# Softmax attention beside a long convolution on one core: groups by quarter of the heads, then by query block

## The chip, the cores and the metric

The kernel runs on one core of a Trainium2 chip. What is measured is device time in microseconds (us) of one launch, from the first to the last instruction with what lies around them; 859.79 us is the median of three runs (858.05 to 861.04). The core has a TensorE (PE) for matmuls into eight PSUM banks, a VectorE (DVE), a ScalarE (ACT), a GpSimd (POOL), a SyncE (SP) that mainly issues transfers, and 16 DMA engines.

## What is computed

Two independent parts write the two halves of the output rows. Part A is attention with 32 heads of 16 channels over 2048 positions; part B is a causal long convolution per channel.

```python
# A: x [2048,512], wqkv [512,1536], wo [512,512]; 32 heads of 16
qkv = (x @ wqkv) -> q, k, v per head
scores = einsum("bhqd,bhkd->bhqk", q, k) * 16 ** -0.5
p = softmax(scores, axis=-1)
o = einsum("bhqk,bhkd->bhqd", p, v)
a = o.reshape(1, 2048, 512) @ wo
# B: q, k, v [2048,512]; shift_k [512,4]; ssm_k [512,2048]; ssm_D [512]
k_shift[s] = sum over m of k[s - m] * shift_k[:, m]
kv = k_shift * v
y = causal convolution of kv with ssm_k along the positions (the reference uses an FFT) + kv * ssm_D
b = q * y
out = concatenate([a, b], axis=-1)
```

## The kernel before

**An order planned while the program is written.** One Python loop at the end of the function runs over steps T. In each step it emits instructions for PE, ACT, DVE, POOL and the DMA queues through objects of class `Eng` and the helper `dma` (its issues all show as L227). Those keep estimated clocks (`pe.t`, `dve.t`, `done`), from which the planner decides what fits where. On the chip the engines follow the order that was written, held only by semaphores: PE, ACT and DVE each run their instructions strictly in that order, so a waiting instruction holds up all behind it.

**Attention.** The 2048 x 2048 scores of each head are cut into blocks of 128 keys x 512 queries: 32 heads x 16 key tiles x 4 query blocks = 2048 blocks. A group is one query block and four heads that sit in the four 32-row strips of PE: 32 groups of 64 blocks. Before, the groups run by query block (`qb`) first and by group of heads (`g`, 8 of them) within it, and the first two groups are interleaved. A step T takes two or three blocks: `emit_qk` puts the score matmuls (L548) into two or three PSUM banks (0 to 2 and 3 to 5 by turns), and ACT takes the exponentials of the step in one instruction (L559) into a ring of five `PT` buffers. Two or three steps later `emit_pv` (L641) multiplies them with the values `VAF`, which carry columns of ones for the softmax sum, and accumulates a group in bank `PVB`. At a group's end DVE transposes it (L705), divides (L712, L716) and, for each pair of groups, transposes back into `OTN` (L729).

**Blocks on DVE.** From step `T_DVE` = 56 on, the third block of a three-bank step may have its exponential on DVE instead (`dve_block`, `exp_on_dve`): one L595, three L602 and one L607, each 128 x 512. The step's ACT instruction is then two blocks wide. A block is only given to DVE when its estimated backlog is at most `BACKLOG` = 3.9 us.

**Projections.** `pe_unit` makes pieces of work in one PSUM bank, emitted in halves, and `evac_unit` copies them out by DVE: `q` (L339, two masked copies L385), `k` (L348, L390), `v` (L368, L414; one key tile for all heads), `kv` (the convolution's shifted and multiplied input, L360, L400). Before, all values, keys and the first query block are projected in the first `N_EARLY` = 184 steps by the list `early`; in these, every second step has two banks only and the units use the free one, bank 5. Later units go to 25 openings of five steps, 21 steps apart from step 190, of which the first, third and fifth step have two banks (`T_SLOT`, `SLOT`, `N_SLOT`, `opens`, `slots`). The number of steps is fixed by this: 184 steps hold 92 x 2 + 92 x 3 = 460 blocks, the openings have 75 two-bank steps, the last 14 blocks go by twos in 7 steps, and the rest needs 475 steps of three, in sum 741.

**Convolution.** `ssm_k` is reversed by DVE (`kz_turn`, L435) and stored to DRAM (`kz_store`). `load_wr` reads from there, for each of 128 quartets of channels, four 128 x 2048 Toeplitz rows of 512 KB into a filter slot of `WR`; there are three slots (`R_W` = 12 rows). `conv_lags` (L815) does up to six lags a step in bank `BGB`, DVE copies the result (L830), PE turns it (L841) and DVE multiplies with q (L850). The transposed loads of `B_k` that `kv` needs are `load_kt(0..2)`; the rows for `load_kt(2)` come free after the last `k` unit.

**Output.** `op_mm`/`op_out` (L760, L769) multiply `OTN` with `WO` and store through POOL's queue. `warm_up` (L1025) adds at most one filler matmul per step, of up to four times 128 columns, where PE would otherwise have been less than `BUSY` = 0.75 busy over the last `WINDOW` = 3.4 us by the planner's clock.

Of the kernel before, what the change touches and what calls it, by code (L numbers as in the profile page):

```python
# [11 lines left out]
S = 2048  # L12
# [9 lines left out]
VROW = 592  # L22
# [7 lines left out]
R_W = 12  # L30
R_PT = 5
R_O = 8
# [4 lines left out]
N_EARLY = 184  # L37
# [21 lines left out]
T_DVE = 56  # L59
T_SLOT = 190  # L60
SLOT = 21
N_SLOT = 25
# [5 lines left out]
BACKLOG = 3.9  # L68
MARGIN = 0.35
EARLY_MARGIN = 0.25  # L70
KV_DUE = 300
# [4 lines left out]
FILL_GAP = 0.25  # L76
RATE = 3.4
# [59 lines left out]
def bass_concat_heads__mha_block__ssm_conv_h3__prompt_kernel(  # L137
# [24 lines left out]
    def sb(name, shape, dt=BF16):  # L162
# [4 lines left out]
    KTo = sb("KTo", [128, 4, S])  # L167
    QTF = sb("QT", [128, 2 * NG * QB + 2 * LEFT])
    QT = QTF[:, 0:2 * NG * QB].rearrange("p (b g f) -> p b g f", b=2, g=NG)
    VAF = sb("VAF", [128, KT, VROW])  # L170
# [9 lines left out]
    WKV = sb("WKV", [128, 8 * D + LEFT])  # L180
    OTN = sb("OTN", [128, R_O, QB])
# [15 lines left out]
    WO = WV  # L197
    VST = [x.rearrange("p (t d) -> p t d", t=NB)
           for x in (WR[:, 8, :], WR[:, 9, :], OUTA[:, :, :].rearrange("p r d -> p (r d)"), VS2[:, :])]
# [3 lines left out]
           QTF[:, NG * QB:NG * QB + LKR].rearrange("p (c s) -> p c s", c=1),  # L203
           WKV[:, 4 * D:4 * D + LKR].rearrange("p (c s) -> p c s", c=1)]
    KT_OF = [(0, 0), (0, 1), (1, 0), (2, 0)]
    DG = OTN[:, 4:8, :].rearrange("p t d -> p (t d)").rearrange("p (c m d) -> p c m d", c=4, m=4)
    KZN = [QTF[:, NG * QB:NG * QB + 2 * S].rearrange("p (c s) -> p c s", c=2),
# [53 lines left out]
    d_w = [DmaSem(sem(f"d_w{i}")) for i in range(5)]  # L261
# [19 lines left out]
    h_wv = dma(act, d_w[2], WV, wview[:, :, 2 * D:3 * D])  # L281
    load_x(1)
    h_wq.append(dma(act, d_w[3], WQ[:, :, 128:D], wview[:, :, 128:D], kb=384))
    h_wk.append(dma(act, d_w[4], WK[:, :, 128:D], wview[:, :, D + 128:2 * D], kb=384))
    h_shk = dma(act, d_tap, SHK[:, :, :], B_shift_k.rearrange("(c p) m -> p c m", p=128), kb=4)
# [4 lines left out]
    load_x(2)  # L290
    load_x(3)
    h_vn, h_kt, h_kt0 = [], {}, {}
    for c in range(4):
        src = bass.AP(tensor=v2.tensor, offset=v2[128 * (NB - 1), 128 * c].offset, ap=[[D, 128], [-128 * D, NB], [1, 128]])
        h_vn.append(dma(sp, d_kv[3 + c], VST[c], src, kb=1024))
# [16 lines left out]
    vones = VAF[:, :, 0:H * VW].rearrange("p k (h e) -> p k h e", e=VW)  # L312
    pool.op(lambda e: e.memset(vones[:, :, :, DH:VW], 1.0))
    h_vaf1 = pool.op(lambda e: e.memset(VAF[:, :, H * VW:VROW], 1.0))
# [3 lines left out]

    bank_free = {b: None for b in range(8)}
    h_q, h_k, h_v = {}, {}, {}  # L320
    def unit_deps(u):
        if u[0] == "q":
            return h_x[u[1]] + [h_wq[min(u[2], 1)]]
        if u[0] == "k":
            return h_x[u[2]] + [h_wk[min(u[1], 1)]]
        if u[0] == "kv":
            return [h_kt[KT_OF[u[1]][0]], h_dg[0]]
        return h_x[u[1] // 4] + [h_wv]

    def pe_unit(u, bank, dcs=(0, 1, 2, 3)):  # L330
# [3 lines left out]
        if kind == "q":  # L334
            _, qb, o = u
# [27 lines left out]
        else:  # L363
            _, kt = u
            deps += h_x[kt // 4] + [h_wv]

            def mm(e, dc):
                return e.matmul(PS[:, bank, :], lhsT=xT[:, dc, kt * 128:(kt + 1) * 128], rhs=WV[:, dc, :],  # L368
                                start=(dc == 0), stop=(dc == 3))

        def fn(e):
            ins = None
            for dc in dcs:
                ins = mm(e, dc)
            return ins
        return pe.op(fn, deps, us=(0.105 + mm_us * len(dcs), 0.235 + mm_us * len(dcs)),
                     run=mm_run * len(dcs))

    def evac_unit(u, bank, h):
        kind = u[0]  # L380
        if kind == "q":
            _, qb, o = u
            for par in range(2):
                hh = h_q[(qb, 2 * o + par)] = urgent(
                    lambda e, par=par: e.tensor_scalar(QT[:, qb % 2, 2 * o + par, :], PS[:, bank, :], MASK[:, par:par + 1], None, ALU.mult),  # L385
                    [h, h_mask] + ([h_kzt[0], h_kvm[0]] if qb == 1 else []), us=V512)
        elif kind == "k":
            _, o, sc = u
            c0 = KEYS0 if (o, sc) == (0, 0) else 0
            hh = urgent(lambda e: e.tensor_copy(KTo[:, o, sc * 512 + c0:(sc + 1) * 512], PS[:, bank, c0:512]), [h],  # L390
                        us=(0.335, 0.46) if c0 else V512)
            h_k[(o, sc)] = hh
            if (o, sc) == (3, 3):
                load_kt(2, h)
        elif kind == "kv":
# [6 lines left out]
            if sum(kv_n[0:2]) == 8 and c < 2:  # L402
                load_qn(0, [h])
                wr_free.append((2, hh))
                load_wr()
            if c == 2 and kv_n[c] == 4:
                h_kvm[0] = h
            if c == 3 and kv_n[c] == 4:
                h_kvm[1] = h
        else:  # L410
            _, kt = u
            dst = VAF[:, kt, 0:H * VW].rearrange("p (h e) -> p h e", e=VW)[:, :, 0:DH]
            src = PS[:, bank, :].rearrange("p (h e) -> p h e", h=H)
            hh = urgent(lambda e: e.tensor_copy(dst, src), [h, h_vaf1], us=V512)  # L414
            h_v[kt] = hh
# [23 lines left out]
    def kz_store(us):  # L439
# [3 lines left out]
        wr_free.extend([(i, h_kzw[0]) for i in range(2)])  # L443
# [35 lines left out]
    for par in range(2):  # L479
        h_q[(0, par)] = bank_free[6] = dve.op(  # L480
            lambda e, par=par: e.tensor_scalar(QT[:, 0, par, :], PS[:, 6, :], MASK[:, par:par + 1], None, ALU.mult),
            [h, h_mask], us=V512)
# [4 lines left out]
    opens = {T + i: T for T in range(T_SLOT, T_SLOT + N_SLOT * SLOT, SLOT) for i in range(5)}  # L487
# [3 lines left out]
    while left_:  # L491
        T = len(banks_of)
        n = 2 if T % 2 == 1 and T < N_EARLY or T in slots else 3
# [7 lines left out]
    def blk(i):  # L501
        s = i % 4
        if i < 8 * KT:
            return 0, (i // 8) % 2, 2 * (i // 16) + (i // 4) % 2, s
        kt = (i // 4) % KT
        g = (i // (4 * KT)) % NG
        qb = i // (4 * KT * NG)
        return qb, g, kt, s

    last_blk = {}  # L510
    for i in range(NBLK):
        qb, g, kt, s = blk(i)
        last_blk[qb * NG + g] = i

    def pvb(n):
        return BGB if n == 1 else PVB
# [3 lines left out]
    def blk_group(i):  # L520
        qb, g, kt, s = blk(i)
        return qb * NG + g

    on_dve = {}
# [3 lines left out]
    def emit_qk(T):  # L528
# [11 lines left out]
        for b, bank in zip(bl, banks):  # L540
            qb, g, kt, s = blk(b)
            deps += [h_q[(qb, g)], h_k[(g // 2, kt // 4)] if g > 1 or kt * 128 >= KEYS0 else h_k0, bank_free[bank]]

        def fn(e):
            ins = None
            for b, bank in zip(bl, banks):
                qb, g, kt, s = blk(b)
                ins = e.matmul(PS[:, bank, :],  # L548
                               lhsT=KTo[32 * s:32 * s + 32, g // 2, kt * 128:(kt + 1) * 128],
                               rhs=QT[32 * s:32 * s + 32, qb % 2, g, :],  # L550
                               start=True, stop=True, tile_position=(32 * s, 0))
            return ins
        h = pe.op(fn, deps, us=(0.33, 0.462), run=0.22)
        if extra is not None:
# [13 lines left out]
    def dve_block(T):  # L568
        if len(banks_of[T]) < 3 or T < T_DVE or T >= NT - N_TAIL - TAIL_GAP:
# [12 lines left out]
        if len(ahead) < 4 * KT - AHEAD + 1 or (n // NG, n % NG) not in h_q or (n % NG // 2, 0) not in h_k:  # L582
# [6 lines left out]
    def exp_on_dve(b, bank, h):  # L589
# [10 lines left out]
        def horner(j, us):  # L600
            src = frac if j == 0 else eh
            st["h"] = dve.op(lambda e: e.scalar_tensor_tensor(eh, src, (A3, A2, A1)[j], frac, ALU.add, ALU.mult),  # L602
                             [st["h"], h_last.get(i - R_EH), h_mul[1]], us=us)

        def last(us):
# [5 lines left out]
                      lambda: (i < R_EH or i - R_EH in h_last) and 1 in h_mul)]  # L611
# [7 lines left out]
    pv_done = {}  # L619
    pt_left = {T: len(b) for T, b in enumerate(banks_of)}  # L620

    def emit_pv(bl, T, again):
        deps = [h_blk[b] for b in bl] + [h_v[blk(b)[2]] for b in bl]
        runs = []
        for b in bl:
            qb, g, kt, s = blk(b)
            n = qb * NG + g
            k = pv_n.get((n, s), 0)
            pv_n[(n, s)] = k + 1
            if k == 0:  # L630
                deps.append(bank_free[pvb(n)])
# [3 lines left out]
            h = 8 * (g // 2) + 2 * s + (g % 2)  # L635
            runs.append((PS[32 * s:32 * s + 32, pvb(n), :], VAF[:, kt, h * VW:h * VW + 32], rhs, k, s))

# [15 lines left out]
        for b in bl:  # L653
            n = blk_group(b)
            if n not in pv_done and all(pv_n.get((n, s)) == KT for s in range(4)):
                pv_done[n] = T
                ends.append(n)
# [5 lines left out]
    def pv_step(T):  # L663
# [4 lines left out]
        for n in ns:  # L668
            if n > 1 and pv_done.get(n - 1, T) >= T:
                break  # L670
            if n == 2 and pv_done.get(0, T) >= T:
                break
            a = [b for b in acts if blk_group(b) == n and blk(b)[2] in h_v]
# [10 lines left out]
            while bl:  # L684
                run = []
                for b in bl:
                    if blk(b)[3] not in [blk(x)[3] for x in run]:
# [10 lines left out]
    def finish_group(n, h, T):  # L698
        qb, g = n // NG, n % NG
        last = n == NQB * NG - 1  # L700
        dt = EH[:, 0, :] if n == 1 else DT[:, :]
        p = n // 2
        dtn = DTN[:, p % 2, :]
        before = [h_mul.get(n - 2 if n == 2 else n - 1)] if n != 1 else []
        h_t = urgent(lambda e: e.transpose(out=dt, in_=PS[:, pvb(n), :]), [h] + before, slack=0.1, us=(0.63, 0.751))  # L705
        bank_free[pvb(n)] = h_t
# [13 lines left out]
        def turn_back(i0, i1, us):  # L720
            sl = slice(128 * i0, 128 * i1)
            deps = [h_mul[2 * p], h_mul[2 * p + 1]]
            if p >= R_O:
                deps += [h_op[((p - R_O) // 4, t)] for t in range(4)]
            if p == 4:
                deps.append(h_kvm[0])
            if p == 7:
                deps.append(h_kvm[1])
            h_otn[(p, i1)] = h_otn[p] = dve.op(lambda e: e.transpose(out=OTN[:, p % R_O, sl], in_=dtn[:, sl]), deps, us=us)  # L729

        def may_turn():
            return 2 * p in h_mul and 2 * p + 1 in h_mul and (p != 7 or kv_n[3] == 4) and (p < R_O or all(((p - R_O) // 4, t) in h_op for t in range(4)))
# [12 lines left out]
    h_op = {}  # L745
# [4 lines left out]
    def load_wop(h_last):  # L750
        h_wop[0] = dma(pool, d_wo, WO, A_wo.rearrange("(o p) f -> p o f", p=128), [h_last])
# [366 lines left out]
```

## Time and profile before

| | |
|---|---|
| median of three runs | 859.79 us (858.05 to 861.04) |
| the profiled execution | span 863.2 us, 3.4 us above the median |
| exponentials on ACT (L559) | 741 instructions, 1834 blocks: 353 of three, 387 of two, one of one |
| exponentials on DVE | 214 blocks, first L595 at 72.6 us, last at 842.4 us |
| first / last L559 | begins 8.76 us / ends 856.2 us |
| DVE | 785.5 us busy |
| first convolution matmul (L815) | 95.3 us |
| first filter load issued | 42.6 us |
| filter loads | 512 of 512 KB |

The page of a profile lists busy time by engine, a strip of 40 equal slices of the span, the chain of waits that ended last, and groups of instructions by source line. Busy times of neighbouring instructions overlap at their ends, so a mean duration is longer than the distance from start to start. "Idle before" is how long the engine had nothing to do ahead of a group, with the instruction that ended the wait. Matmul ends are modelled.

### The profile page before, as it was taken

The page shows a single profiled execution, that of the slowest core. Times are in us where ns is not written, and L with a number is a line of the kernel's source. Part 1 is how long each engine was busy: PE and PEld are TensorE (multiplying, and loading weights), DVE is VectorE, ACT ScalarE, POOL GpSimd, SP SyncE. Part 2 cuts the span into 40 slices and gives each one's busy share as a digit, 9 for nine tenths or more (in the row PEclk, how much of TensorE's full clock was granted, in tenths as well). Part 3 has the DMA queues.
Part 4 walks back from the last instruction along what each step waited for, and adds up shares of the span by engine and source line. Part 5 has one row for each costly group of instructions (what it writes and reads, how often), then busy time and mean ns, then how long its engine had stood idle before and what let it go on. Part 6 is the DMA issues. An engine that isn't in the chain of part 4 may idle for free.

```text
span 863.2 us, 29400 instructions
## 1 busy us (share of the span) xinstructions
PE 750.6 (87%) x13177; PEld 303.9 (35%) x13177; DVE 785.5 (91%) x1335; ACT 836.5 (97%) x746; POOL 17.4 (2%) x34
## 2 busy tenths in 40 slices
PE   8988999998888898888888888888988888888887
PEld 2223333443333333333333333333333333333332
DVE  2428899999889999999999989999999999999994
ACT  6999899999889999999999989999999999999997
POOL 2000000000000000000000000000000000000000
PEclk9999799999989999999999989999999999999999
DMA  9950188989979999999999999999999999999952
GB/s 272 260 206 1 53 305 291 305 273 376 376 296 361 375 410 389 353 406 407 380 376 402 407 376 358 379 368 389 387 408 407 400 394 390 388 407 408 383 211 74
DMA packets 104845, 289.36 MB, mean 335 GB/s; under 512 B 35216, under 2 KB 37264, under 8 KB 104336
## 3 DMA queue, kind: packets, MB, share of 16 engines
q1 hardware_dynamic: 99600, 279.48, 86.8%
q0 software_dynamic: 1808, 6.29, 2.2%
q8 instruction: 104, 1.70, 0.8%
q10 hardware_dynamic: 3312, 1.71, 0.7%
q14 instruction: 21, 0.17, 0.1%
HBM read 276.83 MB, written 6.42 MB: 328 GB/s over the span
## 4 chain that ended last, share of the span: by engine, by line
ACT 72%; DVE 12%; PE 10%; DMA 5%; issue 1%; SPq 1%
ACT PT L559 71%; DMA WR<-kz_scratch 5%; DVE EH L602 5%; PE PS L548 3%; DVE FX L595 2%; PE PS L641 2%; DVE PTD L607 2%; PE PS L815 1%; DVE QT L385 1%; PE PS L368 1%; SPq L227 1%; PE PS L461 1%; PE PS L760 0%; DVE DT L705 0%; PE PS L348 0%
## 5 line engine op out<-in xcount | busy, mean ns | idle before, releaser
L559 ACT ACTIVATE PT<-PS 128x1536 bf16<-128x1536 f32 (+1 forms) x741 | 833.5, 1376 | 14.7 <-PE PS L548 14.2
L548 PE MATMUL PS<-QT,KTo 32*128 32x512 bf16 x2048 | 308.3, 390 | 93.8 <-ACT PT L559 78.5
L602 DVE SCALAR_TENSOR_TENSOR EH<-EH,FX 128x512 f32<-128x512 f32 x428 | 283.1, 681 | 0.1
L815 PE MATMUL PS<-WR,KV 128*14 128x128 bf16 (+15 forms) x8192 | 220.3, 222 | 4.8 <-DMA WR<-kz_scratch 4.5
L641 PE MATMUL PS<-PT,VAF 128*32 128x512 bf16 x1834 | 203.7, 395 | 5.3 <-DVE DT L705 4.4
L815 PEld LDWEIGHTS PS<-WR,KV 128*8 128x8 bf16 (+15 forms) x8192 | 150.3, 88 | 86.8 <-issue 42.6
L548 PEld LDWEIGHTS PS<-QT,KTo 32*128 32x128 bf16 x2048 | 73.1, 91 | 274.5 <-ACT PT L559 232.9
L595 DVE TENSOR_SCALAR FX<-PS 128x512 f32<-128x512 f32 x214 | 146.4, 684 | 4.9 <-PE PS L548 4.3
L607 DVE SCALAR_TENSOR_TENSOR PTD<-EH,FX 128x512 uint16<-128x512 f32 x214 | 144.4, 679 | 0.0
L602 DVE SCALAR_TENSOR_TENSOR EH<-FX 128x512 f32<-128x512 uint16 x214 | 143.3, 684 | 0.0
L641 PEld LDWEIGHTS PS<-PT,VAF 128*32 128x32 bf16 x1834 | 49.0, 93 | 127.5 <-issue 111.3
L1025 PE MATMUL PS<-IDN,ZW 128*32 128x512 bf16 (+3 forms) x222 | 71.9, 324 | 0.0
L641 PE MATMUL PS<-PTD,VAF 128*32 128x512 bf16 x214 | 60.0, 392 | 0.0
L414 DVE CAST VAF<-PS 128x512 bf16<-128x512 f32 x16 | 11.1, 692 | 29.2 <-PE PS L368 29.2
L705 DVE STREAM_TRANSPOSE DT<-PS 128x512 f32<-128x512 f32 x31 | 22.1, 712 | 11.1 <-PE PS L641 10.9
L385 DVE TENSOR_SCALAR QT<-PS,MASK 128x512 bf16<-128x512 f32 x30 | 21.0, 742 | 5.1 <-PE PS L339 5.1
L1025 PEld LDWEIGHTS PS<-IDN,ZW 128*32 128x32 bf16 x222 | 21.4, 96 | 11.3 <-issue 10.4
L830 DVE CAST YB<-PS 128x512 bf16<-128x512 f32 x32 | 21.8, 682 | 0.7 <-PE PS L815 0.5
L760 PE MATMUL PS<-WKV,OTN 128*128 128x512 bf16 x64 | 20.1, 392 | 0.3 <-DVE OTN L729 0.3
L368 PE MATMUL PS<-WKV,xT 128*128 128x512 bf16 x64 | 18.8, 384 | 1.8 <-DVE VAF L414 1.2
L348 PE MATMUL PS<-xT,WKV 128*128 128x512 bf16 (+1 forms) x64 | 18.9, 392 | 0.5 <-DVE VAF L414 0.5
L339 PE MATMUL PS<-xT,WQ 128*128 128x512 bf16 x60 | 18.7, 400 | 0.1
(69 smaller groups left out, 198.6 us busy)
## 6 DMA issues: line engine op xcount, KB each, us to landing
WR<-kz_scratch SPq DMA_DIRECT2D x512, 512.0 KB, 7.8
kz_scratch<-WR SPq DMA_DIRECT2D x1, 2176.0 KB, 8.3
QN<-in_B_q_dram POOLq DMA_DIRECT2D x2, 1024.0 KB, 12.0
out_dram<-QN POOLq DMA_DIRECT2D x2, 1024.0 KB, 8.4
out_dram<-OUTA POOLq DMA_DIRECT2D x12, 128.0 KB, 5.2
QN<-in_B_ssm_k_dram SPq DMA_DIRECT2D x1, 1024.0 KB, 6.3
QT<-in_B_ssm_k_dram SPq DMA_DIRECT2D x1, 1024.0 KB, 8.2
WR<-in_B_v_dram SPq DMA_DIRECT2D x2, 512.0 KB, 7.5
```

Of the source, the lines that this page charges most:

```text
L368: return e.matmul(PS[:, bank, :], lhsT=xT[:, dc, kt * 128:(kt + 1) * 128], rhs=WV[:, dc, :], start=(dc == 0), stop=(dc == 3))
L385: lambda e, par=par: e.tensor_scalar(QT[:, qb % 2, 2 * o + par, :], PS[:, bank, :], MASK[:, par:par + 1], None, ALU.mult),
L548: ins = e.matmul(PS[:, bank, :], lhsT=KTo[32 * s:32 * s + 32, g // 2, kt * 128:(kt + 1) * 128], rhs=QT[32 * s:32 * s + 32, qb % 2, g, :], ...
L559: h_exp[T] = act.op(lambda e: e.activation(PT[:, T % R_PT, 0:n * QB], PS[:, banks[0]:banks[0] + n, :].rearrange("p b f -> p (b f)"), ACT.E ...
L595: h_f = urgent(lambda e: e.tensor_scalar(fx, PS[:, bank, :], FIX_ADD, FIX_HI, ALU.add, ALU.min), [h, h_last.get(i - R_FX)], slack=0.6)
L602: st["h"] = dve.op(lambda e: e.scalar_tensor_tensor(eh, src, (A3, A2, A1)[j], frac, ALU.add, ALU.mult), [st["h"], h_last.get(i - R_EH), h_ ...
L607: lambda e: e.scalar_tensor_tensor(out16, eh, A4, fx, ALU.mult, ALU.add),
L641: ins = e.matmul(dst, lhsT=w, rhs=rhs, start=(k == 0), stop=(k == KT - 1), tile_position=(0, 32 * s))
L705: h_t = urgent(lambda e: e.transpose(out=dt, in_=PS[:, pvb(n), :]), [h] + before, slack=0.1, us=(0.63, 0.751))
L815: ins = e.matmul(PS[32 * c:32 * c + NB - n, BGB, 128 * (kk % 4):128 * (kk % 4) + 128], lhsT=KV[:, qd, n:NB, c], rhs=WR[:, r + c, 128 * (NB ...
L830: hh = urgent(lambda e: e.tensor_copy(YB[:, half, :].rearrange("p (k i) -> p k i", k=4), src), [h, h_yb[0]], slack=0.3, us=V512)
L1025: pe.op(lambda e: e.matmul(PS[32 * s:32 * s + 32, pvb(n), 0:128 * k], lhsT=ZW[:, :], rhs=rhs, start=False, stop=False, tile_position=(0, 3 ...
```

## The change

Groups now run by quarter of the heads (`o`, eight heads with 128 channels), then by query block, two groups (`par`) to each pair (`PAIRS`); the last two quarters are interleaved over the query blocks. Keys and values are held for two quarters (`KTo[:, o % 2]`, `VA[:, o % 2]`), queries for three pairs (`R_Q`), and `OTN` has all 16 tiles. A `v` unit is now one quarter of the values for four key tiles: 16 matmuls of 128 columns instead of 4 of 512. Blocks may go to DVE from step 4; there are no two-bank steps before step 68 (`N_OPEN`), where units use bank 7 (`BGB`), and from 68 on there are 40 openings 16 steps apart. In the steps of an opening that still has a unit to do, no block goes to DVE. All of `x` is loaded ahead of `ssm_k`; the convolution starts at step 68 with four filter slots, all convolution input of the first two quarters being made before. The filler may add several matmuls in one step while PE has been less than `LOW` = 0.55 busy. Some transfers' costs in the planner (`kb`) are other numbers.

```diff
-VROW = 592
+VROW = 160
-R_W = 12
+R_W = 16
-R_O = 8
+R_Q = 3
-N_EARLY = 184
+N_OPEN = 68
-T_DVE = 56
-T_SLOT = 190
-SLOT = 21
-N_SLOT = 25
+T_DVE = 4
+SLOT = 16
+N_SLOT = 40
-BACKLOG = 3.9
+BACKLOG = 4.5
+LOW = 0.55
...
-    KTo = sb("KTo", [128, 4, S])
-    QTF = sb("QT", [128, 2 * NG * QB + 2 * LEFT])
-    VAF = sb("VAF", [128, KT, VROW])
+    KTo = sb("KTo", [128, 2, S])
+    QT = sb("QT", [128, R_Q, 2, QB])
+    VA = sb("VA", [128, 2, KT, VROW])
...
-    h_wv = dma(act, d_w[2], WV, wview[:, :, 2 * D:3 * D])
+    h_wv = [dma(act, d_w[2], WV[:, :, 0:128], wview[:, :, 2 * D:2 * D + 128], kb=128)]
     load_x(1)
+    load_x(2)
+    load_x(3)
+    h_shk = dma(act, d_tap, SHK[:, :, :], B_shift_k.rearrange("(c p) m -> p c m", p=128), kb=4)
     h_wq.append(dma(act, d_w[3], WQ[:, :, 128:D], wview[:, :, 128:D], kb=384))
     h_wk.append(dma(act, d_w[4], WK[:, :, 128:D], wview[:, :, D + 128:2 * D], kb=384))
-    h_shk = dma(act, d_tap, SHK[:, :, :], B_shift_k.rearrange("(c p) m -> p c m", p=128), kb=4)
+    h_wv.append(dma(act, d_w[5], WV[:, :, 128:D], wview[:, :, 2 * D + 128:3 * D], kb=384))
     kzview = B_ssm_k.rearrange("(p c) s -> p c s", c=4)
...
-    load_x(2)
-    load_x(3)
...
+    PAIRS = [(o, qb) for o in (0, 1) for qb in range(4)]
+    PAIRS += [(2, 0), (2, 1), (2, 2), (3, 0), (3, 1), (3, 2), (2, 3), (3, 3)]
+    OF = [PAIRS[n // 2][0] for n in range(NQB * NG)]
+    LAST = {o: max(n for n in range(NQB * NG) if OF[n] == o) for o in range(4)}
...
+            _, o, sc = u
+            deps += h_x[sc] + [h_wv[min(o, 1)]]
+            mm_us, mm_run = 0.27, 0.21
+
+            def mm(e, j):
+                ins = None
+                for dc in range(4):
+                    ins = e.matmul(PS[:, bank, 128 * j:128 * j + 128], lhsT=xT[:, dc, (4 * sc + j) * 128:(4 * sc + j + 1) * 128],
+                                   rhs=WV[:, dc, o * 128:(o + 1) * 128], start=(dc == 0), stop=(dc == 3))
+                return ins
...
         load_kt(1, h_kzt[0])
-        wr_free.extend([(i, h_kzw[0]) for i in range(2)])
+        load_kt(2, h_kzt[0])
+        wr_free.extend([(i, h_kzw[0]) for i in range(R_W // 4 - 1)])
         load_wr()
...
-    opens = {T + i: T for T in range(T_SLOT, T_SLOT + N_SLOT * SLOT, SLOT) for i in range(5)}
+    opens = {T + i: T for T in range(N_OPEN, N_OPEN + N_SLOT * SLOT, SLOT) for i in range(5)}
     slots = {T for T in opens if (T - opens[T]) % 2 == 0}
...
-        n = 2 if T % 2 == 1 and T < N_EARLY or T in slots else 3
+        n = 2 if T in slots else 3
...
     def dve_block(T):
-        if len(banks_of[T]) < 3 or T < T_DVE or T >= NT - N_TAIL - TAIL_GAP:
+        if len(banks_of[T]) < 3 or T in opens and (part[0] or next_unit(T)) or T < T_DVE or T >= NT - N_TAIL - TAIL_GAP:
             return None
...
-    early = [(2, ("v", 0)), (3, ("v", 1)), (4, ("k", 0, 0)), (8, ("v", 2)), (9, ("v", 3)), (10, ("k", 0, 1)), (13, ("v", 4)),
...
+    early = [(0, ("k", 0, 0)), (1, ("v", 0, 0)), (4, ("k", 0, 1)), (6, ("v", 0, 1)), (9, ("k", 0, 2)), (11, ("v", 0, 2)),
+             (14, ("k", 0, 3)), (17, ("v", 0, 3)), (32, ("q", 1))]
+    units = [("kv", c, i) for c in range(2) for i in range(4)] + [(x, 1, i) for i in range(4) for x in "kv"]
+    early += [(N_OPEN - 5 - 2 * (len(units) - i), u) for i, u in enumerate(units)]
+
+    def step(n):
+        return NT * n // (NQB * NG)
+
+    jobs = [(step(2 * p) - 8, ("q", p)) for p in range(2, 16)]
+    jobs += [(step(OF.index(o)) - 16 + 4 * sc, (x, o, sc)) for o in (2, 3) for sc in range(4) for x in "kv"]
+    jobs += [(step(5 + 4 * c), ("kv", c + 2, i)) for c in range(2) for i in range(4)]
+    jobs += [(step(25 + 2 * qb) + 8 * t, ("op", qb, t)) for qb in range(NQB - 1) for t in range(4)]
...
+        while live:
+            gap = at(h_exp[T - 1]) + 0.14 - pe.t - FILL_GAP
...
+            if lately > LOW * WINDOW:
+                return
```

## The prediction

> **What bounds the kernel now.** I read the page's busy times first, then what ACT waited for, then windows of time. The execution has a span of 863.2 us; the median shown is 859.8, so differences from this profile are taken off 859.8.
>
> ```profile
> PE 750.6 (87%) x13177; PEld 303.9 (35%) x13177; DVE 785.5 (91%) x1335; ACT 836.5 (97%) x746; POOL 17.4 (2%) x34
> L559 ACT ACTIVATE PT<-PS 128x1536 bf16<-128x1536 f32 (+1 forms) x741 | 833.5, 1376 | 14.7 <-PE PS L548 14.2
> L559 ACT ACTIVATE PT<-PS 128x1536 bf16<-128x1536 f32 x353 | 533.4, 1600 | 7.8 <-PE PS L548 7.6
> L559 ACT ACTIVATE PT<-PS 128x1024 bf16<-128x1024 f32 x387 | 417.0, 1174 | 6.9 <-PE PS L548 6.6
> ```
>
> ACT sets the end: its exponentials run from 8.8 to 856.2 us and fill all but 14.7 us of that, nearly all of it waits for score matmuls. A third block costs 1600 - 1174 = 426 ns. 1834 blocks are then 781 us, and the rest of 833.5, 52 us over 741 instructions, is 0.070 us for each instruction. So the end moves in three ways: fewer blocks on ACT, fewer instructions, less waiting.
>
> The windows (columns: us, then busy of PE, weight loads, DVE, ACT, POOL, granted clock, DMA share, GB/s) say where.
>
> ```profile
> 0.00:20.00 20.00, 16.76 (x90) 5.22 (x90) 4.63 (x10) 13.06 (x13) 4.94 (x14) 1.00 1.00 275
> 20.00:40.00 20.00, 18.00 (x119) 4.94 (x116) 8.40 (x14) 19.59 (x18) 0.24 (x2) 1.00 1.10 270
> 40.00:60.00 20.00, 17.98 (x123) 4.62 (x121) 4.32 (x7) 20.00 (x19) 0.00 (x0) 1.00 0.77 251
> 60.00:80.00 20.00, 17.17 (x129) 5.15 (x127) 14.40 (x25) 20.00 (x20) 0.00 (x0) 1.00 0.00 1
> 80.00:100.00 20.00, 18.63 (x173) 7.29 (x171) 18.03 (x30) 17.87 (x18) 0.00 (x0) 0.77 0.01 2
> 200.00:220.00 20.00, 15.48 (x273) 6.27 (x272) 18.14 (x32) 17.35 (x17) 0.77 (x1) 0.92 1.00 374
> 240.00:260.00 20.00, 17.86 (x293) 6.42 (x293) 17.38 (x29) 17.61 (x17) 0.00 (x0) 0.83 0.78 289
> 700.00:740.00 40.00, 35.17 (x695) 14.51 (x696) 40.00 (x70) 40.00 (x36) 1.08 (x2) 1.00 1.02 388
> ```
>
> DVE is as full as ACT once it takes blocks (40.00 of 40 near the end), but nearly idle before 70 us. And ACT waits where the granted clock falls: 2.1, 2.6 and 2.4 us in the three windows at 0.77, 0.92 and 0.83. The mean clock is 0.980; in the finest windows it is either 1.00 or 0.50, so some 863.2 x 0.020 x 2 = 35 us ran at half clock, and they hold most of ACT's 14.2.
>
> **The change, part by part.**
>
> *DVE from step 4.* A block's five DVE operations start 0.6 us apart (0.57 + 1.80 + 0.60 in the chain):
>
> ```profile
> 446.61 0.57 DVE FX L595
> 447.18 1.80 DVE EH L602 x3
> 448.98 0.60 DVE FX L595
> 449.58 0.60 DVE PTD L607
> ```
>
> So a block is 3.0 us of DVE and takes 0.426 from ACT. Step 4 comes near 8.8 + 4 x 1.35 = 14.2 us. From 14 to 80 us DVE was busy 1.35 (14 to 20) + 8.40 + 4.32 + 14.40 = 28.5 of 66 us, 37.5 free: room for 12.5 blocks, 5.3 us of ACT. Copies there stay as many: 16 values, 4 first keys, two queries and some 4 more keys before; 8 values, 8 keys, 2 queries and 8 `kv` after. Bounds 0 and 5.3; I take 11 blocks, 4.7 us, since the window is nearly all usable.
>
> *Fewer steps.* 68 steps of three hold 204 blocks, 40 openings have 120 two-bank steps with 240, the tail 14 in 7; the other 1590 need 530 steps. 68 + 120 + 530 + 7 = 725, 16 fewer: 16 x 0.070 = 1.1 us.
>
> *PE in the opening.* The units for the first two quarters stand two steps apart from step 31 to 61. The trace prices them by starts (us, us):
>
> ```profile
> 83.94 0.39 PE L548 MATMUL PS<-QT,KTo 32*128 32x512 bf16 x3 [0.34 <-ACT PT L559]
> 84.27 0.62 PE L360 MATMUL PS<-OTN,QN 128*128 128x128 bf16 x8
> 84.86 0.39 PE L548 MATMUL PS<-QT,KTo 32*128 32x512 bf16 x2
> ```
>
> Scores 0.33, half a `kv` unit 0.59; four-matmul halves are 0.54 (67.09 to 67.63), value products 0.33. A new `v` half is eight 128-column matmuls like the `kv` one, so 0.59 too. In 33 steps: 33 x 0.72 (scores, values, some DVE blocks' values apart) = 23.8, eight `kv` and four `v` at 1.18 and four `k` at 1.08 = 18.5, in sum 42.3 us. ACT needs 33 x 1.35 = 44.6, less ten DVE blocks 40.3. PE is 2.0 us over, and ACT waits that long: -2.0, between 0 (DVE takes fewer) and 5 (the half clock comes on top). Elsewhere the longer `v` units (0.1 us each) lie under ACT.
>
> *Half clock and late filters.* The filler may now repeat within a step; a fourth slot and other transfer costs change when filters come. What that does to the 14.2 us, no row shows: 0 to 14.2. I take 5, two thirds of the 7.1 at 80 to 100, 200 to 220 and 240 to 260, which lie where the order is new. The first of these begins without a stop of PE:
>
> ```profile
> 86.00:88.00 2.00, 1.40 (x14) 1.00 0.00 0
> 88.00:90.00 2.00, 1.76 (x14) 1.00 0.00 0
> 90.00:92.00 2.00, 2.00 (x16) 0.67 0.00 0
> 92.00:94.00 2.00, 2.00 (x18) 0.50 0.00 0
> ```
>
> PE was busy 3.16 of 4 us and lost half its clock all the same (columns: PE busy, clock, DMA). The Trainium skill, "TensorE: Matmul & The Clock Gate", Part 1, has the gate fall after an idle window of about 3.4 us; this trace disagrees on what counts as idle. By the page there is no such gap here to fill and this term would be nothing, an estimate of 855 to 857 us. The trace decides.
>
> *Openings.* 40 instead of 25, and no block to DVE while one has a unit left: five steps, 3 x 0.92 + 2 x 1.35 = 5.5 us without a new block. Cost taken: nothing. The cover is DVE's own queue: between first operations of blocks at 598.15 and 604.15 us it worked through 6.0 us without a gap, on queued blocks, a transpose and a YB copy. Without cover, see the slower rival.
>
> *Moved loads.* On SP `x` 2 and 3 (9.1 us of issue) now stand before `ssm_k`, so turns, k transposes and filters come some 6 us later: first k transpose issued near 34 instead of 28.0, landing by 42 to 48; the first `kv` unit at step 31, near 47. The three filters then issue from about 49 instead of 42.6 and land by 67 at 400 GB/s, under the empty stretch to step 68 (near 93 us, before 95.3). Cost 0; without cover PE stands at `kv` up to 5 us with scores queued behind. ACT's one more issue, under 0.9 us, lies in its 1.6 us wait before L483. On POOL's queue (POOL 2% busy) the load of `WO` (512 KB) moves from step 184 to behind the last `k` unit, near step 494, and is first needed near step 566; the first q load (1 MB) moves ahead of the convolution, when no filter is awaited. Both move the same bytes as before: 0.
>
> *Filter bandwidth.* 268.4 MB at the 407 GB/s of the long windows are 660 us, with 730 to run: no bound. The Trainium skill, "DMA: Bandwidth & Descriptors", Bandwidth, gives 358 GB/s per core where both cores of a pair stream; that would make 750 us and the filters the end, for no gain. The trace exceeds it.
>
> *Sum.* 4.7 + 1.1 - 2.0 + 5.0 = 8.8. Each us off the end also takes 1/3.0 block from DVE, 0.14 us: 8.8 / 1.14 = 7.7. 859.8 - 7.7 = **852.1 us**. Its own range: (4.3 + 1.1 + 2 - 3) / 1.14 = 3.9 to (5.3 + 1.1 + 9 - 1) / 1.14 = 12.6, so 847 to 856.
>
> **Rivals.** *All waits go.* Filler and fourth slot keep clock and filters: 14.2 instead of 5, opening 1: 19.0 / 1.14 = 16.7, **843 us**. For it: the waits sit at few places; against: some are filters late at 203 and 484 us. With the full DVE gain and no opening loss it reaches 842.
>
> *The k transposes are late.* PE stands 5 us at `kv`, then half clock costs 2.5 as at 90 us: (8.8 - 7.5) / 1.14 = 1.1, **858.7**, no change. For it: one queue, each step 6 us later; against: a margin of up to 5 us.
>
> *DVE runs dry in the openings.* If its queue is 2.7 us short in each of 40: 108 us, 36 blocks, 15.3 us of ACT: (8.8 - 15.3) / 1.14 = -5.7, **865.5**. It makes the kernel slower by 0.3% from 2.1 us per opening (84 us of DVE). For it: 200 of 725 steps are opening steps; before, two of five admitted blocks. Against: the 6.0 us bridged, and a backlog limit of 4.5.
>
> **How the numbers follow.** Forecast 0.49, all waits go 0.17, transposes late 0.12, DVE dry 0.22. About 0.3%, 2.6 us, is what runs of this kernel can tell from no change: faster 0.66, same 0.12, slower 0.22. The range takes the fast rival's end, 842, and goes to 866.
>
> **What would show it.** First L595 near 15 us; 725 instructions at L559; DVE blocks 222 or so (fewer than 195: DVE dry, with DVE idle after 100 us); L559's wait for L548 near 11 us, a third of it before 95; PE standing at L360 before 50 us would be the late transpose. The prediction is wrong if DVE is not full after step 68, or if the half-clock stretches grow.

## The result, and the profile after

The changed kernel takes 854.18 us in the median of eight runs (851.27 to 855.99), beside 859.16 us for the kernel before on the same chip (eight runs, 856.62 to 863.04): a ratio of 0.9931, 95% interval 0.9908 to 0.9955. The forecast was 852.1 us, with 847 to 856 as its own range. The profiled execution has a span of 853.7 us and took 855.4.

The page of the changed kernel; first busy times, then the shares of the chain that ended last, then the groups that answer to those shown of before (L575 was L559, L611 was L595):

```profile
PE 733.1 (86%) x13362; PEld 311.1 (36%) x13399; DVE 811.6 (95%) x1375; ACT 831.1 (97%) x730; POOL 17.6 (2%) x34
ACT 81%; DVE 11%; PE 7%; issue 1%
L575 ACT ACTIVATE PT<-PS 128x1024 bf16<-128x1024 f32 (+1 forms) x725 | 828.2, 1385 | 9.8 <-PE PS L559 9.5
L611 DVE TENSOR_SCALAR FX<-PS 128x512 f32<-128x512 f32 x222 | 152.3, 688 | 2.9 <-PE PS L559 2.6
```

725 instructions instead of 741, 222 blocks on DVE instead of 214, and DVE 95% busy instead of 91%. The chain has no share of DMA any more; before, late filters had 5% of it (in a second profile of the kernel before 3%). The windows show where DVE got its blocks (columns as before: us, busy of PE, weight loads, DVE, ACT, POOL, clock, DMA share, GB/s):

```profile
0.00:20.00 20.00, 15.76 (x107) 6.51 (x110) 8.33 (x16) 12.32 (x12) 4.72 (x14) 1.00 1.07 214
20.00:40.00 20.00, 16.27 (x146) 5.58 (x148) 19.80 (x35) 20.00 (x17) 0.76 (x3) 0.95 0.98 231
40.00:60.00 20.00, 18.91 (x196) 9.07 (x191) 19.09 (x33) 19.08 (x17) 0.00 (x0) 0.88 1.11 318
60.00:80.00 20.00, 17.32 (x178) 7.58 (x178) 19.65 (x34) 20.00 (x17) 1.32 (x1) 1.00 0.88 324
80.00:100.00 20.00, 17.71 (x163) 6.24 (x161) 18.53 (x33) 18.47 (x16) 0.00 (x0) 0.83 0.00 1
700.00:740.00 40.00, 35.42 (x660) 14.28 (x661) 39.40 (x67) 40.00 (x37) 2.16 (x4) 1.00 0.97 360
```

From 20 us on DVE is as full as ACT, where it had 8.40, 4.32 and 14.40 of each 20 us before. Near the end nothing is different.

### The profile page after: what moved, and what is told of

Same layout as the page of the kernel before. It is cut to its first block, busy times and chain, and to the rows that moved or that the text cites. A ratio compares the mean times of both kernels' runs of the same rounds, so it can differ in the third digit from the quotient of the medians.

```text
span 853.7 us, 29793 instructions
## 1 busy us (share of the span) xinstructions
PE 733.1 (86%) x13362; PEld 311.1 (36%) x13399; DVE 811.6 (95%) x1375; ACT 831.1 (97%) x730; POOL 17.6 (2%) x34
## 4 chain that ended last, share of the span: by engine, by line
ACT 81%; DVE 11%; PE 7%; issue 1%
ACT PT L575 81%; DVE EH L618 4%; PE PS L559 2%; DVE PTD L623 2%; DVE FX L611 1%; PE PS L655 1%; DVE QT L408 1%; PE PS L484 1%; PE PS L357 1%; PE PS L766 1%; PE PS L820 0%; DVE DT L716 0%; PE PS L378 0%; PE PS L366 0%; DVE KTo L414 0%
## 5 line engine op out<-in xcount | busy, mean ns | idle before, releaser
L575 ACT ACTIVATE PT<-PS 128x1024 bf16<-128x1024 f32 (+1 forms) x725 | 828.2, 1385 | 9.8 <-PE PS L559 9.5
L559 PE MATMUL PS<-QT,KTo 32*128 32x512 bf16 x2048 | 296.6, 387 | 95.9 <-ACT PT L575 79.1
L618 DVE SCALAR_TENSOR_TENSOR EH<-EH,FX 128x512 f32<-128x512 f32 x444 | 294.2, 686 | 0.7
L820 PE MATMUL PS<-WR,KV 128*9 128x128 bf16 (+15 forms) x8192 | 223.5, 220 | 1.3 <-issue 0.9
L655 PE MATMUL PS<-PT,VA 128*32 128x512 bf16 x1826 | 200.5, 392 | 5.4 <-DVE DT L716 4.6
L820 PEld LDWEIGHTS PS<-WR,KV 128*16 128x16 bf16 (+15 forms) x8192 | 147.3, 87 | 96.2 <-issue 58.6
L559 PEld LDWEIGHTS PS<-QT,KTo 32*128 32x128 bf16 x2048 | 71.4, 91 | 257.5 <-ACT PT L575 222.4
L611 DVE TENSOR_SCALAR FX<-PS 128x512 f32<-128x512 f32 x222 | 152.3, 688 | 2.9 <-PE PS L559 2.6
L655 PEld LDWEIGHTS PS<-PT,VA 128*32 128x32 bf16 x1826 | 47.9, 93 | 119.9 <-issue 102.1
L655 PE MATMUL PS<-PTD,VA 128*32 128x512 bf16 x222 | 67.1, 386 | 0.0
L389 PE MATMUL PS<-WKV,xT 128*128 128x128 bf16 x256 | 18.8, 220 | 0.8 <-DVE QN L855 0.5
L389 PEld LDWEIGHTS PS<-WKV,xT 128*128 128x128 bf16 x256 | 14.4, 98 | 7.5 <-issue 4.7
```

What stands on the lines that cost most here:

```text
L389: ins = e.matmul(PS[:, bank, 128 * j:128 * j + 128], lhsT=xT[:, dc, (4 * sc + j) * 128:(4 * sc + j + 1) * 128], rhs=WV[:, dc, o * 128:(o + ...
L559: ins = e.matmul(PS[:, bank, :], lhsT=KTo[32 * s:32 * s + 32, OF[n_] % 2, kt * 128:(kt + 1) * 128], rhs=QT[32 * s:32 * s + 32, n_ // 2 % R ...
L575: h_exp[T] = act.op(lambda e: e.activation(PT[:, T % R_PT, 0:n * QB], PS[:, banks[0]:banks[0] + n, :].rearrange("p b f -> p (b f)"), ACT.E ...
L611: h_f = urgent(lambda e: e.tensor_scalar(fx, PS[:, bank, :], FIX_ADD, FIX_HI, ALU.add, ALU.min), [h, h_last.get(i - R_FX)], slack=0.6)
L655: ins = e.matmul(dst, lhsT=w, rhs=rhs, start=(k == 0), stop=(k == KT - 1), tile_position=(0, 32 * s))
L820: ins = e.matmul(PS[32 * c:32 * c + NB - n, BGB, 128 * (kk % 4):128 * (kk % 4) + 128], lhsT=KV[:, qd, n:NB, c], rhs=WR[:, r + c, 128 * (NB ...
```

## The experiments

Levels are given as ratios to the kernel before, timed beside each run on the same chip, with the 95% interval in brackets; the changed kernel is 0.993. Differences in us are between medians.

**The kernel before, profiled again.**

> The kernel before once more, for a second profile. Theory 1 (the profile on record was a long execution, its span 863.2 us against 857.5 for the median run, less the 1.7 us that lie around a span): the same 741 exponentials and 214 DVE blocks, ACT busy 833 to 834 us, but ACT's wait for score matmuls 8 to 11 us instead of 14.2 and the mean granted clock above 0.983. Theory 2 (the kernel before really waits 14 us): the wait is again 13 us or more, and the span above 861.

Span 856.4 us, clock 0.992:

```profile
L559 ACT ACTIVATE PT<-PS 128x1536 bf16<-128x1536 f32 (+1 forms) x741 | 832.1, 1381 | 8.4 <-PE PS L548 8.1
```

The same program waited 8.1 us instead of 14.2. Over 61 timed executions of it (854.8 to 865.6 us; eleven more lie on the same line) time goes with the mean granted clock: a straight line gives 854.6 us at full clock (standard error 0.4) and 5.0 us more for each 0.01 below, with a correlation of 0.88; the median clock is 0.989. An execution takes 1.7 us more than its span, so the one on record took some 864.9 us, 5 us above the median and not 3.4, and was near the longest. That is theory 1.

**The changed kernel, profiled and timed again.**

> The changed kernel once more on the chip of this call, as the level for the others. Theory 1 and the rival alike: ratio 0.991 to 0.996 to the kernel before, 222 blocks, ACT's wait for score matmuls 7 to 11 us.

0.9929 (0.9908 to 0.9949), 222 blocks, a wait of 8.8 us. Its 14 executions lie on a line of 850.7 us at full clock (standard error 0.7) and 4.1 us for each 0.01; the median clock is 0.992.

**Blocks on DVE from step 56 again, in the new order.**

```diff
-T_DVE = 4
+T_DVE = 56
```

> The changed kernel with one number undone: blocks go to DVE from step 56 instead of 4. Theory 1 (blocks on DVE in the first 80 us are the gain): some 13 blocks return to ACT, 222 become 209 to 212; 11 x 0.426 / 1.14 = 4.1 us, so the ratio to the kernel before is 0.997 to 1.001 where the changed kernel has 0.993. Rival (the waits for a cold PE and late filters are the gain): 0.992 to 0.995, no more than 1.5 us above the changed kernel.

1.0041 (1.0021 to 1.0060): 9.5 us above the changed kernel, twice what was expected, and slower than the kernel before. The direction is that of theory 1, the size beyond its range.

```profile
L575 ACT ACTIVATE PT<-PS 128x1024 bf16<-128x1024 f32 (+1 forms) x725 | 834.7, 1415 | 12.0 <-PE PS L559 11.6
L611 DVE TENSOR_SCALAR FX<-PS 128x512 f32<-128x512 f32 x208 | 141.6, 682 | 6.4 <-PE PS L559 5.8
```

14 blocks fewer on DVE and 6.2 us more of ACT, so the early blocks are the gain and the new order without them is a loss. ACT waits 2.8 us longer as well (11.6 for 8.8 in the second profile). The clock is not the reason: its median was 0.994, above the changed kernel's.

**Early blocks in the old order.** The groups keep their order; the second group's transpose gets a buffer of its own, so that DVE's blocks no longer wait for it, and DVE may start at step 4.

```diff
-T_DVE = 56
+T_DVE = 4
...
+    DT1 = sb("DT1", [128, QB], FP32)
...
-        dt = EH[:, 0, :] if n == 1 else DT[:, :]
+        dt = DT1[:, :] if n == 1 else DT[:, :]
```

> The kernel before, in its old order, with blocks on DVE from step 4; the first groups get a transpose buffer of their own, so that DVE's ring is free for them. Theory 1 (early DVE blocks are the gain, the order of the groups is not): 220 to 225 blocks on DVE, ratio 0.993 to 0.996. Rival (the old order has no room: every second early step has two banks, and its 20 early copies and 16 projections crowd PE and DVE): under 218 blocks or ACT's wait above 14 us, ratio 0.998 or more.

225 blocks on DVE, 11 more than before, and no gain: 1.0013 (0.9990 to 1.0036). That is the rival by the ratio alone: it had asked for under 218 blocks or a wait above 14 us, and ACT's wait was 12.2. The groups of instructions that fell between 14 and 80 us show where it goes. In the kernel before (second profile):

```profile
L559 ACT ACTIVATE PT<-PS 128x1024 bf16<-128x1024 f32 (+1 forms) x60 | 67.0, 1318 | 0.5 <-PE PS L548 0.4
L548 PE MATMUL PS<-QT,KTo 32*128 32x512 bf16 x147 | 22.9, 384 | 5.1 <-ACT PT L559 3.1 <-DVE KTo L390 1.0
L595 DVE TENSOR_SCALAR FX<-PS 128x512 f32<-128x512 f32 x3 | 2.0, 679 | 0.0
```

In the old order with early blocks:

```profile
L560 ACT ACTIVATE PT<-PS 128x1024 bf16<-128x1024 f32 (+1 forms) x60 | 63.4, 1189 | 3.8 <-PE PS L549 3.7
L549 PE MATMUL PS<-QT,KTo 32*128 32x512 bf16 x150 | 23.0, 384 | 5.1 <-ACT PT L560 2.3 <-DVE KTo L391 2.2
L596 DVE TENSOR_SCALAR FX<-PS 128x512 f32<-128x512 f32 x13 | 8.9, 682 | 0.8 <-PE PS L549 0.8
```

In the changed kernel:

```profile
L575 ACT ACTIVATE PT<-PS 128x1536 bf16<-128x1536 f32 (+1 forms) x54 | 65.8, 1354 | 0.9 <-PE PS L559 0.9
L559 PE MATMUL PS<-QT,KTo 32*128 32x512 bf16 x162 | 22.9, 402 | 5.4 <-ACT PT L575 5.2
L611 DVE TENSOR_SCALAR FX<-PS 128x512 f32<-128x512 f32 x17 | 11.6, 684 | 0.1
```

The count of score matmuls is the progress. In the old order ten more blocks on DVE gave at most three more in all (150 for 147): ACT did the same 60 steps, each shorter, and waited 3.7 us for PE. In the new order 54 steps carry 162 blocks. The clock does not explain it: in this window it was 1.00 in both profiles of the old order and 0.95 in the changed kernel.

**The old order with all of the change's rules for DVE.** To the kernel above come `BACKLOG` 4.5 and the exclusion of blocks from openings with work.

> The kernel before, in its old order, with all the rules of the change for DVE: blocks from step 4, none in an opening that still has a unit to do, BACKLOG 4.5. Theory 1 (the old order has no place for early blocks: two-bank steps in the opening, three filter slots): 221 blocks but ACT's wait stays above 10 us, ratio 0.998 to 1.003. Rival (the missing exclusion was what took back the gain in the old order): ACT's wait 9 us or less, ratio 0.993 to 0.996.

0.9997 (0.9972 to 1.0022), 221 blocks. Theory 1 by time; its wait of over 10 us did not come in the profiled execution, which at 855.3 us was the shortest of twelve (8.2 us of waiting, which the rival had asked for, at a clock of 0.996). 3.7 us of that wait lay between 14 and 80 us, as in the run above, and PE stood 5.9 us for filters (4.5 in the run above, 4.5 and 2.2 in the two profiles of the kernel before). How much of the lost gain each of the two took is not shown.

**The old opening's two-bank steps in the new order.**

```diff
-        n = 2 if T in slots else 3
+        n = 2 if T in slots or T % 2 == 1 and T < N_OPEN else 3
```

> The changed kernel with one thing of the old opening put back: until step 68 every second step has two banks (34 x 2 + 34 x 3 = 170 blocks there, 736 steps in all). Theory 1 (early blocks on DVE pay in the new order because its opening has only three-bank steps, in which PE has time for a unit): ACT waits 3 us or more for score matmuls between 14 and 80 us, as in the old order with early blocks (3.7), against 0.4 to 0.9 in the changed kernel; with 11 instructions more (0.8 us) the ratio to the kernel before is 0.997 or more. Rival (the width of the early steps does not matter, the old order failed for its late filters alone): that wait stays under 1.5 us, ratio 0.992 to 0.995.

1.0113 (1.0079 to 1.0146). Between 14 and 80 us:

```profile
L575 ACT ACTIVATE PT<-PS 128x1024 bf16<-128x1024 f32 (+1 forms) x58 | 60.8, 1128 | 6.9 <-PE PS L559 6.6
L559 PE MATMUL PS<-QT,KTo 32*128 32x512 bf16 x140 | 22.2, 384 | 2.8 <-ACT PT L575 1.8 <-DVE KTo L414 0.9
L611 DVE TENSOR_SCALAR FX<-PS 128x512 f32<-128x512 f32 x17 | 11.7, 689 | 1.1 <-PE PS L559 1.0
```

The same 17 blocks on DVE, and 140 blocks done instead of 162, with the clock at 1.00. That is theory 1 as to the width of the steps. Its reason is in part argued: in a two-bank step ACT is done in 2 x 0.426 + 0.070 = 0.92 us, while scores, values and half a unit are 1.2 us of PE by the starts shown in the prediction. But PE also stood 5.9 us for copies of a full DVE in this window (2.7 in the second profile of the changed kernel), and the two were not separated. The loss is larger than ACT's 6.6 us here, since the shifted plan also waits 5.4 us after 800 us, where the clock was 0.86; what brought that on was not looked into. Three-bank steps in the opening of the old order were not tried, so that its two-bank steps are why early blocks gained nothing there is likely and not shown.

**Blocks on DVE in openings.** The exclusion is taken out of `dve_block`.

```diff
-        if len(banks_of[T]) < 3 or T in opens and (part[0] or next_unit(T)) or T < T_DVE or T >= NT - N_TAIL - TAIL_GAP:
+        if len(banks_of[T]) < 3 or T < T_DVE or T >= NT - N_TAIL - TAIL_GAP:
```

> The changed kernel, but blocks may go to DVE in an opening that still has a unit to do. Theory 1 (the exclusion only starves DVE): 230 blocks on DVE instead of 222, 8 x 0.426 / 1.14 = 3 us faster than the changed kernel, ratio to the kernel before 0.988 to 0.991. Rival (the exclusion keeps DVE's queue short for the copies of the openings; with blocks there the copies come late, PE stands and ACT with it): about as many blocks more, but ACT's wait for score matmuls rises from 9 to over 14 us, ratio 0.996 or more.

230 blocks, eight more, and 13.9 us slower (13 by the ratios): 1.0084 (1.0055 to 1.0112). ACT waited 21.4 us, 12.6 more than in the second profile of the changed kernel. The waits of PE for DVE (us, times, longest) in the second profile of the changed kernel,

```profile
PE PS L655 <- DVE DT L716: 4.6, 12, 0.7
PE PS L766 <- DVE OUTA L775: 2.0, 3, 1.0
PE PS L766 <- DVE QN L855: 0.5, 2, 0.3
```

and here:

```profile
PE PS L655 <- DVE DT L716: 7.1, 14, 1.1
PE PS L766 <- DVE OUTA L775: 3.2, 5, 1.3
PE PS L766 <- DVE QN L855: 2.4, 2, 1.3
PE PS L366 <- DVE QT L408: 2.0, 1, 2.0
```

All waits of this kind add up to 17.0 us there and 30.8 here, 13.8 more, about as much as the time. A bank that a unit or a group of values has filled is free only when DVE has copied or transposed it, and that now queues behind five-operation blocks; the next matmul for the bank waits at the head of PE with score matmuls behind it. That is the rival.

**Three filter slots.**

```diff
-R_W = 16
+R_W = 12
...
-DMA_KB = 396
+DMA_KB = 407
```

> The changed kernel with three filter slots instead of four (and 407 instead of 396 KB per us for the planner, without which three slots don't fit its plan). Theory 1 (the fourth slot is why no filter is late in the changed kernel): PE waits at L820 for filters by 2 us or more, ACT's wait rises by 2 to 5 us, ratio to the kernel before 0.996 to 1.000. Rival (the planner's new transfer costs do it, the slot is only reserve): no such wait, ratio 0.992 to 0.995.

1.0076 (1.0051 to 1.0100), 13.7 us above the changed kernel with 222 blocks as there. That is theory 1, at more than its price: ACT waited 18.5 us, and PE stood for filters.

```profile
PE PS L820 <- DMA WR<-kz_scratch: 16.9, 21, 2.7
```

**Its control: four slots, 407 KB per us.**

> The control for the run with three slots: the changed kernel with four slots and the same 407 KB per us in the planner. Theory 1 (the third slot less was the loss there, not the number): no wait for filters above 1 us at L820, ratio to the kernel before 0.990 to 0.996. Rival (407 makes the plan run ahead of the real filters): waits at L820 of 5 us or more, ratio above 1.000.

0.9949 (0.9924 to 0.9974), and PE never stood for a filter. So it is the slot, at 1.0076 - 0.9949 = 1.3%, 11 us, against this control. Four slots in the old order were not tried: they need 16 KB more in each partition, and the room comes from the regrouping (by the shapes, keys 16 to 8 KB, values 18.5 to 10, queries 16 to 6, outputs 8 to 16).

**One filler per step.** `LOW` is 0, so that the loop ends after one matmul.

> The changed kernel with at most one filler matmul in a step, as in the kernel before. Theory 1 (repeated fillers hold the clock): more time at half clock, mean granted clock under 0.985 instead of 0.990, ACT's wait 2 to 5 us longer, ratio to the kernel before 0.995 to 0.999. Rival (the filler's rule does not matter): clock 0.988 to 0.995, ratio 0.991 to 0.995, and PE a few us less busy.

0.9931 (0.9900 to 0.9962), median clock 0.991 for 0.992. That is the rival; PE was 731.8 us busy in the profile, where the changed kernel's two profiles have 733.1 and 739.7. It is a weak test of fillers: there are 239 of them instead of 253, so the repeats that it forbids are few.

**The old costs of POOL's transfers in the planner.** The four `kb` numbers go back to 512 and 128.

> The changed kernel with the planner's old costs for the four kinds of transfer on POOL's queue (512 or 128 KB instead of 1780, 1860, 1600 and 535). Theory 1 (the new costs keep the plan behind the real filters): filters come late after those transfers, PE waits 2 us or more at L820, ACT's wait rises by 2 to 5 us, ratio to the kernel before 0.996 to 1.000. Rival (four slots absorb it): no wait at L820 above 1 us, ratio 0.991 to 0.994.

Below the changed kernel too by the median: 851.94 us, 0.9895 (0.9868 to 0.9922). Filters do come late now and then (PE stands 3.3 us at L820), but ACT waited 5.2 us in the profiled execution and the median clock is 0.996. Neither as written: theory 1 has the late filters but not their price, and the rival, nearer in time, had 0.991 to 0.994 and no such wait.

**The same with a shorter tail.** `TAIL_GAP` is 2.

> The changed kernel with the old costs of POOL's transfers in the planner, and blocks on DVE until two steps later (TAIL_GAP 2 instead of 4). Theory 1 (with the old costs the gain of the run before holds, and DVE has one more block to take in its 8 us of idle time at the end): 223 blocks, ACT's wait 5 to 8 us, ratio to the kernel before 0.986 to 0.991. Rival (the gain of the old costs was chance of that plan and of those executions): ACT's wait 9 us or more, ratio 0.992 or more.

852.28 us, 0.9925 (0.9901 to 0.9950), 223 blocks, a wait of 7.4 us: theory 1 by the wait, the rival by the ratio. By medians both are some 2 us under the changed kernel's 854.2 and 854.5; by the intervals, which overlap, that is likely and not settled, and the shorter tail shows nothing.

## Why the prediction was right, and where it was not

**What bounds it** held: ACT, by blocks, by instructions and by waits. At full clock the two lines above give 854.6 and 850.7, a gain of 3.9 us (standard error 0.8); the forecast's terms without clock and filters were 4.7 + 1.1 - 2.0 = 3.8, or 3.3 with the correction. That the two agree so well is partly luck: the 3.9 contain what late filters cost before, and the terms are off in both directions, as the next points show.

**DVE from step 4** was right in mechanism, a little small in its early part: by 96 us 20 blocks against 7, so 13 instead of 11, from 15.2 us on. Over the whole kernel 222, as said, eight more than before; the five between are likely given back by the shorter run (5 / 3.0, an estimate of 1.7) and by the openings (lifting the exclusion gave eight blocks). The condition was missing: the same early blocks gained nothing in the old order and with two-bank steps. I had the 0.72 us of scores and values and the 0.5 to 0.6 us of half a unit, but applied them to the new opening alone.

**Fewer steps**: 725 as computed. With 8 x 0.426 = 3.4 the two terms make 4.5 us of ACT; measured 832.1 - 828.2 = 3.9 against the second profile of the kernel before, 5.3 against the first.

**PE in the opening**, 2.0: ACT waited 0.9 and 1.5 us between 14 and 80 us in two profiles, 0.4 before. The term is about half of what I took, or less.

**Half clock and late filters**, 5.0, is the mis-sized term. It came from one execution's 14.2 us, and that execution was 5 us above the median; a second one waited 8.1, the changed kernel 9.5 and 8.8. What is left over many executions is a clock of 0.992 for 0.989. By the two lines that makes 860.1 and 854.0 us, 6.1 apart, of which 6.1 - 3.9 = 2.2 go with the clock; by the measured differences of 5.0 and 5.6 us it is 1 to 2. The filler's repeats had no visible part in it. Late filters did: the fourth slot holds them off (PE stood 4.5 and 2.2 us for filters before, 0 after), and without it the change would be a loss. The forecast had no row for that slot, which was worth 11 us against its control in this plan.

**Openings**, 0, held as a sum (DVE was 704 of 720 us busy from 100 to 820 us, 705 before), and the slower rival's price had the sign wrong: the exclusion does not starve DVE, it keeps copies in time, and taking it out cost 13.9 us. **Moved loads**, 0, held: the first k transpose was issued at 34.9 us, the filters from 49.9 (forecast near 34 and 49), the first `kv` matmul ran at 41.5 without a wait for it; PE stood 0.6 us for `x` 1, 1.6 in the second profile. The first filter was used at 96.4.

**All waits go** did not happen in the changed kernel; the nearest, the old transfer costs, reached 849.7 us in its best run at clock 0.998.

The Trainium skill, "TensorE: Matmul & The Clock Gate", Part 1, says that the gate's window runs freely, so that one and the same kernel has a different number of cold matmuls at its start from run to run. These runs vary too, with clocks of 0.981 to 0.998 for one program, but not at the start alone: in the first profile the clock was 1.00 up to 90 us and 0.50 from 92 us, in the second 1.00 from 80 to 100 us. The page puts the cost of the ramp, the warm-up, at under 1% of a span; the 865.6 - 854.8 = 10.8 us, 1.3%, between shortest and longest execution here are of another kind.

## What to carry to other kernels

When a second engine shares a load, ask not only whether it is idle but whether the producer of both can keep their joint pace at that place: idle time of DVE was worth 9.5 us in one opening and nothing in another. A full engine that also frees another's buffers should get no long work where those copies are due. And take a term for waits from several executions: a single profile can be near the longest of sixty.

## What was not expected of the hardware

One program's time goes with its share of half clock, 5.0 us for each 0.01 of mean clock (61 runs, correlation 0.88). If all that is lost is lost at 0.50, as in the finest windows but for their edges, 0.01 is 17 us at half clock: an estimate of 0.3 us lost for each us. Plans with the same 222 blocks had median clocks from 0.984 (three slots) to 0.996 (old transfer costs). What makes the clock fall in one plan and not in the other was not settled. The profiled number of fillers does not order them (239 with three slots, 245 with the old costs, 253 in the changed kernel), but it was never varied by much.
